# Three chunks in two layers: chunk 0 alone, then chunks 1 and 2 together with seven block products for eight

## The chip, the cores and the metric

The kernel runs on one NeuronCore of one Trainium2 chip. The metric is the device time of one execution in microseconds (us); the time before is the median of three runs. Everything about the insides of an execution comes from one profiled execution of the kernel before.

## What is computed

Block attention with a window and block summaries, followed by two feed-forward layers, all in float32:

```python
x = attention(q, k, v)                    # as (1536 tokens, 512)
g, val = x @ w_gate, x @ w_val            # 512 -> 1536, twice
y = (g * sigmoid(g) * val) @ w_out        # 1536 -> 512
h = y @ w_in                              # 512 -> 2048
out = where(h >= 1, h, where(h <= -1, 0, (h + 1)**2 / 4)) @ w_out2   # 2048 -> 512
```

The attention has batch 2, 8 heads, 768 positions of 64 numbers. The weights arrive as float64 and are decoded on the chip.

## The kernel before

The 1536 tokens are three chunks of 512. A block product takes a 128x128 block of weights (or of the hidden tile) as the stationary operand and 512 columns as the moving one. To keep float32 accuracy each operand is split into a high and a low float32r part, and a block product is three matmuls of 128x512 (high·high, high·low, low·high: `PASSES`, issued by `mm3`, line 888). Per chunk, layer 1 has 12 units f of 128 hidden columns: gate and value products (4 block products each, PSUM tiles `pg`, `pv`), and the output product (`acc_y`, 4 block products). Layer 2 has 16 units: inner (`pi`) and output. That is 816 matmuls of 128x512 per chunk and 2448 in all.

Around the products: two weight units form a pack of 128x1024. A pack is loaded raw (`raw`), decoded on ScalarE and VectorE (`dx`, `dl`, `wb`), written to DRAM in decoded form (`kept_...`), and split into high and low (`wA`, lines 339/343 and 820). Later chunks read the decoded pack back (`wf`) and split it again. Each unit's activation takes ScalarE (tanh or relu, line 925 or 941) and VectorE (lines 931, 936, 955), and its result is split too (`h`). Attention of the later chunks is scattered between the matmuls.

No order is written by hand. A planner (`Plan.emit`) takes jobs with a rank, engine costs, needs and rings of buffers, and issues whichever job can start earliest; the numbers in the table `T` set the ranks, and its `order` says which chunk and layer follow one another: chunk 0 and 1 layer 1, chunk 0 and 1 layer 2, chunk 2 layer 1 and 2. Where the planner expects TensorE to idle in front of a new PSUM bank, `bank` fills in transposes of the identity that nothing reads (line 267), at most ten.

## Time and profile before

| what | value |
|---|---|
| device time, median of 3 runs | 647.35 us (646.94 to 647.78) |
| the profiled execution: device time | 648.05 us |
| the profiled execution: span, first to last instruction | 646.3 us |
| TensorE matmul busy | 634.6 us (98%) |
| VectorE, ScalarE, GpSimd busy | 443.8, 304.4, 46.8 us |
| mean granted TensorE clock | 0.997 |

PE is TensorE's matmuls, DVE is VectorE, ACT ScalarE, POOL GpSimd, SP the engine that issues the DMAs. The profiled execution took 0.70 us more than the median of the runs, and 1.75 us of it lie outside the span.

### The profile page before, as it was taken

How to read it: one execution, taken by the hardware profiler on the slowest of the kernel's cores; microseconds unless marked ns; L12 is line 12 of the kernel's file. 1: busy time of each engine (PE TensorE's matmuls, PEld its weight loads, DVE VectorE, ACT ScalarE, POOL GpSimd, SP SyncE). 2: the span in 40 equal slices, each digit the busy share in tenths (PEclk: the TensorE clock that was granted, in tenths of full speed). 3: DMA queues.
4: the chain of work that ended last, by engine and by line, in shares of the span. 5: the costliest groups of instructions: out<-in, count | busy, mean ns of one | idle time of the engine just before them, and what ended most of it. 6: DMA issues, size and time to landing. Idle time of an engine off the chain costs nothing.

```text
span 646.3 us, 9320 instructions
## 1 busy us (share of the span) xinstructions
PE 634.6 (98%) x3543; PEld 516.0 (80%) x3543; DVE 443.8 (69%) x785; ACT 304.4 (47%) x501; POOL 46.8 (7%) x92
## 2 busy tenths in 40 slices
PE   7999999998999999999999999999999999999997
PEld 6777777776888888888887787778888888888886
DVE  5798978887755568987867667675565555756552
ACT  5696787775422225667644545353322222533332
POOL 7420003222000000000000100000000000000000
PEclk9999999998999999999999999999999999999999
DMA  9999999269523335699722422221523332323201
GB/s 208 277 331 275 371 368 300 92 213 315 218 98 98 98 124 193 239 241 375 276 98 84 161 66 87 95 82 65 188 74 97 98 97 99 112 84 109 87 1 65
DMA packets 78348, 105.99 MB, mean 164 GB/s; under 512 B 36832, under 2 KB 59360, under 8 KB 78304
## 3 DMA queue, kind: packets, MB, share of 16 engines
q1 hardware_dynamic: 78304, 105.40, 51.7%
q8 instruction: 28, 0.46, 0.3%
q14 instruction: 16, 0.13, 0.1%
HBM read 84.41 MB, written 20.97 MB: 163 GB/s over the span
## 4 chain that ended last, share of the span: by engine, by line
PE 91%; DMA 3%; DVE 2%; SPq 1%; ACT 1%; issue 1%; POOL 0%; DVEq 0%; POOLq 0%; ACTq 0%
PE acc_y L888 36%; PE pi L888 20%; PE pg L888 14%; PE pv L888 14%; PE px L505 2%; PE sc L549 1%; DMA kraw<-in_k_dram 1%; DMA kept_g<-wb 1%; PE pt L605 1%; PE pv L423 1%; DMA vrest<-in_v_dram 1%; SPq L363 1%; DVE wb L797 1%; PE pq L489 0%; PE pk L452 0%
## 5 line engine op out<-in xcount | busy, mean ns | idle before, releaser
L888 PE MATMUL acc_y<-wA,h 128*128 128x512 f32 x576 | 140.5, 393 | 0.0
L888 PE MATMUL pi<-y,wA 128*128 128x512 f32 x576 | 139.3, 391 | 0.0
L888 PEld LDWEIGHTS pi<-y,wA 128*128 128x128 f32 x576 | 107.5, 188 | 22.8 <-issue 0.6
L888 PEld LDWEIGHTS acc_y<-wA,h 128*128 128x128 f32 x576 | 107.0, 188 | 22.5 <-issue 0.5
L888 PE MATMUL pg<-x,wA 128*128 128x512 f32 x432 | 108.7, 398 | 1.9 <-POOL wA L820 1.8
L888 PE MATMUL acc_y<-h,wA 128*128 128x512 f32 x432 | 106.1, 394 | 0.6 <-DVE u L936 0.4
L888 PE MATMUL pv<-x,wA 128*128 128x512 f32 x432 | 106.1, 392 | 0.4 <-DVE x L518 0.4
L888 PEld LDWEIGHTS pg<-x,wA 128*128 128x128 f32 x432 | 81.2, 191 | 20.2 <-POOL wA L820 2.2
L888 PEld LDWEIGHTS acc_y<-h,wA 128*128 128x128 f32 x432 | 80.1, 188 | 18.7 <-DVE u L936 0.9
L888 PEld LDWEIGHTS pv<-x,wA 128*128 128x128 f32 x432 | 80.5, 188 | 17.5 <-DVE x L518 0.8
L820 DVE TENSOR_TENSOR wA<-wf,wA 128x1024 fp32r<-128x1024 f32 x68 | 83.4, 1226 | 6.0 <-ACT wA L339 3.7
L339 ACT ACTIVATE wA<-wf 128x1024 fp32r<-128x1024 f32 x37 | 39.3, 1062 | 88.5 <-PE acc_y L888 57.3
L941 ACT ACTIVATE r<-pi,half_b 128x512 f32<-128x512 f32 x48 | 33.0, 688 | 95.7 <-PE pi L888 95.6
L955 DVE SCALAR_TENSOR_TENSOR r<-pi,r 128x512 f32<-128x512 f32 x48 | 33.0, 687 | 29.1 <-ACT r L947 29.0
L925 ACT ACTIVATE u<-pg 128x512 f32<-128x512 f32 x36 | 21.6, 600 | 62.3 <-PE pg L888 62.2
L931 DVE SCALAR_TENSOR_TENSOR u<-u,pg 128x512 f32<-128x512 f32 x36 | 24.7, 686 | 37.3 <-ACT u L925 37.2
L936 DVE TENSOR_TENSOR u<-u,pv 128x512 f32<-128x512 f32 x36 | 24.7, 687 | 33.9 <-PE pv L888 33.7
L797 DVE SCALAR_TENSOR_TENSOR wb<-dx,dl 128x1024 int32<-128x1024 int32 x34 | 41.3, 1221 | 6.6 <-ACT dl L339 2.1
L343 DVE CAST wA<-wf 128x1024 fp32r<-128x1024 f32 x31 | 22.0, 710 | 33.8 <-PE pi L888 27.6
L786 ACT ACTIVATE dx<-raw 128x1024 f32<-128x1024 f32 x34 | 38.6, 1140 | 5.2 <-DVE wb L797 3.2
L341 POOL TENSOR_SCALAR kwin<-kT 128x96 f32<-128x96 f32 (+2 forms) x40 | 17.0, 442 | 315.1 <-PE sc L549 257.4
L820 DVE TENSOR_TENSOR wA<-wb,wA 128x1024 fp32r<-128x1024 f32 x30 | 36.6, 1221 | 0.5
(92 smaller groups left out, 567.1 us busy)
## 6 DMA issues: line engine op xcount, KB each, us to landing
raw<-in_moe_w_out_dram SPq DMA_DIRECT2D x14, 1024.0 KB, 8.7
wf<-kept_g SPq DMA_DIRECT2D x24, 512.0 KB, 3.3
raw<-in_moe_w_in_dram SPq DMA_DIRECT2D x16, 512.0 KB, 6.7
wf<-kept_i SPq DMA_DIRECT2D x16, 512.0 KB, 3.3
wf<-kept_z SPq DMA_DIRECT2D x16, 512.0 KB, 3.2
raw<-in_moe_w_gate_dram SPq DMA_DIRECT2D x12, 512.0 KB, 7.4
raw<-in_moe_w_val_dram SPq DMA_DIRECT2D x12, 512.0 KB, 8.9
kept_g<-wb SPq DMA_DIRECT2D x12, 512.0 KB, 8.6
```

The costliest lines, as they stand in the source:

```text
L339: nc.scalar.activation(out, in_, AF.Copy, scale=scale)
L341: nc.gpsimd.tensor_scalar(out, in_, scale, 1.0, op0=ALU.mult, op1=ALU.mult)
L343: nc.vector.tensor_copy(out, in_)
L786: nc.scalar.activation(x, raws[k][:, :, :, 1].bitcast(F32), AF.Prelu, scale=2.0 ** -112, alpha=2.0 ** 32)
L797: nc.vector.scalar_tensor_tensor(b, x, 3, words.pop((k, "low")), op0=ALU.logical_shift_left, op1=ALU.bitwise_or)
L820: e.tensor_tensor(out, a, b, op=ALU.subtract)
L888: nc.tensor.matmul(dst, lhs(a), rhs(b), start=first and i == 0, stop=last and i == 2)
L925: nc.scalar.activation(u, banks_of[n], AF.Tanh, scale=0.5)
L931: nc.vector.scalar_tensor_tensor(u, u, 1.0, banks_of[n], op0=ALU.add, op1=ALU.mult)
L936: nc.vector.tensor_tensor(u, u, banks_of[n], op=ALU.mult)
L941: nc.scalar.activation(r, banks_of[n], AF.Relu, bias=half_b, scale=0.5)
L955: nc.vector.scalar_tensor_tensor(r, banks_of[n], 1.0, r, op0=ALU.max, op1=ALU.min)
```

## The change

Chunk 0 goes through both layers as before, in the planner's `units`. Meanwhile the attention of chunks 1 and 2 leaves its results as plain float32 tiles (`flat`). Then chunks 1 and 2 go through both layers together. In gate, value and inner a 2x2 arrangement is formed: two 256-row halves of the contraction, two units f, two chunks. Its eight block products become seven, in Winograd's form of Strassen's scheme (`FORMS`): four combinations of weights (`add_group`, tile `sj`) and four of activations (`add_term`, tile `tj`) are formed by VectorE or GpSimd, both get split (`wjo`, `wjs`, `xj`), and seven products per quad (`form`, tiles `qg`, `qv`, `qi`; six matmuls each) are accumulated in PSUM banks. A running sum in one bank is copied out three times on the way (`fork`), each time before the next product is added to it, and three of the copies get another bank added (`join`). The output products keep eight of eight (`row_jobs`); they read their packs again per chunk (tile `dd`).

Matmuls of 128x512: `pg`, `pv` and `pi` had 432, 432 and 576. Now chunk 0 keeps 144, 144 and 192, and the joint part has 12 gate and value quads and 8 inner quads of 42 matmuls.

To make room, twenty-two 128x512 slots (`s0` to `s21`) replace several pools, `dx` and `dl` share one ring `dd`, PSUM is four banks `b0` to `b3` and four accumulators, and the attention's tiles share memory (`big0`, `big1`) with the split activations of the joint part, which can therefore be written only when all attention is done.

```diff
- 'order': ((0, 1), (1, 1), (0, 2), (1, 2), (2, 1), (2, 2)),
...
+ 'order': ((0, 1), (0, 2)),
...
+    FORMS = {
+        1: ("o", 1, 0), 2: ("o", 2, 1), 3: ("s", 3, 2), 4: ("o", 0, 6),
+        5: ("s", 0, 3), 6: ("s", 1, 4), 7: ("s", 2, 5),
+    }
...
+    SUMS = {0: (0, 1, ALU.add), 2: (2, 0, ALU.subtract), 1: (4, 2, ALU.subtract), 3: (3, 5, ALU.subtract)}
...
+        for s, (x, y, _) in SUMS.items():
+            needs = [("ja", *n)] + [("js", *n, z - 4) for z in (x, y) if z >= 4]
+            job(("js", *n, s), {"DVE+": 0.7, "POOL": 1.32}, t + T["js"][st - 1],
+                lambda e, *_, s=s: add_group(st, i, s, e), needs, (("raw",),) if s == 0 else (),
+                follows=[("js", *n, 0)] if s == 2 else [])
...
+    TERMS = {
+        3: ((C2, 0), (C1, 0)), 5: ((C2, 1), (C2, 0)), 4: ((C2, 1), 3), 6: ((C1, 1), 4),
+    }
...
+    def add_term(st, k, b, engine, ring):
+        x, y = (
+            parts_of[st, k, z] if isinstance(z, int) else flat[st, z[0], k + HALF * z[1]]
+            for z in TERMS[b])
+        t = parts_of[st, k, b] = slot(ring, "tj")
+        (nc.gpsimd if engine == "POOL" else nc.vector).tensor_tensor(t, x, y, op=ALU.subtract)
...
+    def term_hi(st, k, b, engine):
+        if (st, k) not in xts:
+            xts[st, k] = big.tile([P, 7, 2, CH], F32R, tag=f"big{k}", name=f"xj{k}")
+        copy(engine, xts[st, k][:, b, 0], operand(st, k, b))
...
+    def term_lo(st, k, b, engine):
+        t = xts[st, k]
+        subtract(engine, t[:, b, 1], operand(st, k, b), t[:, b, 0].bitcast(F32))
...
+        for b in range(7):
+            c, z = ((C1, 0), (C1, 1), (C2, 1))[b] if b < 3 else (None, None)
+            source = ("f", st, c, k + HALF * z) if b < 3 else ("t", st, k, b)
+            job(("th", st, k, b), {"ACT": 0.64, "DVE+": 0.43}, t + T["th"] + b / 3,
+                lambda e, b=b: term_hi(st, k, b, e), [source, *before])
+            job(("tl", st, k, b), {"DVE+": 0.7, "POOL": 1.32}, t + T["tl"] + b / 3,
+                lambda e, b=b: term_lo(st, k, b, e), [("th", st, k, b)], (),
+                [(source, 0)])
+
+    def form(q, p, first, last, ring=None):
+        st, i, e = q
+        what, x, y = FORMS[p]
+        if ring:
+            quads[q, "acd"[{1: 0, 2: 2, 5: 1}[p]]] = bank(ring, "q" + "gvi"[e if st == 1 else 2])
+        dst = quads[q, {2: "d", 5: "c", 3: "c"}.get(p, "a")]
+        w = split[what, st, i, e]
+        for k in range(HALF):
+            t = xts[st, k]
+            mm3(dst, lambda a: w[:, a, x, k * P:(k + 1) * P], lambda b: t[:, y, b],
+                first and k == 0, last and k == HALF - 1, skip_group_check=not first)
+
+    def fork(q, what, engine, ring):
+        t = quads[q, what] = slot(ring, "q" + what)
+        copy(engine, t, quads[q, "a"])
+
+    def join(q, what, src):
+        nc.vector.tensor_tensor(quads[q, what], quads[q, what], quads[q, src], op=ALU.add)
+
+    def quad_jobs(q, t, slots):
+        st, i, e = q
+        order = dict(zip((1, 2, 6, 5, 7, 4, 3), T["qp"]))
+        waits = {6: [("qf", *q, "s1")], 7: [("qf", *q, "u2")], 4: [("qf", *q, "u3")],
+                 3: [("qj", *q, "u3")]}
+        for p, dt in order.items():
+            what, _, y = FORMS[p]
+            needs = [("gl", what, *q)] + [("tl", st, k, y) for k in range(HALF)] + waits.get(p, [])
+            if p == 1 and q in follow:
+                needs.append(("qp", *follow[q], 1))
+            last = {"o": 4, "s": 3}[what] == p
+            gives = [(("gh", what, *q), 0)]
+            job(("qp", *q, p), {"PE": 6 * MM}, t + dt,
+                lambda eng, *ring, p=p: form(q, p, p in (1, 2, 5), True, *ring),
+                needs, (QB,) if p in (1, 2, 5) else (), gives)
+        for p, what in ((1, "s1"), (6, "u2"), (7, "u3")):
+            job(("qf", *q, what), {"ACT": 0.61, "DVE": 0.7}, t + order[p] + T["qf"],
+                lambda eng, ring, what=what: fork(q, what, eng, ring), [("qp", *q, p)], (slots,))
+        for what, src, p, gives in (
+                ("s1", "d", 2, [(("qp", *q, 2), 0)]), ("u3", "c", 5, []),
+                ("u2", "c", 3, [(("qp", *q, 5), 0)])):
+            job(("qj", *q, what), {"DVE": 0.7}, t + order[p] + T["qj"],
+                lambda eng, what=what, src=src: join(q, what, src),
+                [("qp", *q, p), ("qf", *q, what)], (), gives)
...
+        for c, df, made, key, held in (
+                (C1, 1, ("qj", *q, "s1"), "s1", (("qf", *q, "s1"), 0)),
+                (C2, 0, ("qj", *q, "u3"), "u3", (("qf", *q, "u3"), 0)),
+                (C1, 0, ("qp", *q, 4), "a", (("qp", *q, 1), 0)),
+                (C2, 1, ("qj", *q, "u2"), "u2", (("qf", *q, "u2"), 0))):
+            act_jobs(kind, (c, st, f + df), lambda key=key: quads[q, key], t, made, held, slots,
+                     "DVE" if key == "a" else "DVE+")
...
+    def row_jobs(c, st, f, t):
+        kind, n = "oz"[st - 1], f - f % PACK
+        key = (kind, n, c)
+        if f == n:
+            r = t + T["rw"]
+            job(("f32", key), {"DMA": (0.35, 0.7 * PACK)}, r, lambda *_: read_rows(key),
+                [("keep", kind, n)], (("wf",),), follows=prior("f32", key) or [("bits", len(packs) - 1)])
+            split_jobs(key, r + T["rs"], ("f32", key), "dd")
+        split_hidden((c, st, f), t + T["rh"])
+        parts = [(m,) for m in range(KK)] if f == LAST[st] else [(0, 1), (2, 3)]
+        for i, ms in enumerate(parts):
+            name = ("row", c, st, f, i)
+            gives = []
+            if i == len(parts) - 1:
+                gives = [(("hh", c, st, f), 0)] + ([(("hi", key), 0)] if f > n else [])
+            job(name, {"PE": 3 * MM * len(ms)}, t + i * 2.6 / len(parts),
+                lambda e, *rings, ms=ms: row_use(key, c, st, f, ms, rings),
```

The order of the rows on the engines is the planner's, and so it can't be read off the diff. Three places follow.

TensorE in layer 1 before, in chunk 2: one unit f, with four block products of gate (`pg`), four of value (`pv`) and four of output (`acc_y`), each over the four blocks `x` of the contraction; x3 is the three passes.

```order
L888 MATMUL pg<-x_3491,wA 128x512 x3
L888 MATMUL pg<-x_3763,wA 128x512 x3
L888 MATMUL pg<-x_3978,wA 128x512 x3
L888 MATMUL pg<-x_4206,wA 128x512 x3
L888 MATMUL pv<-x_3491,wA 128x512 x3
L888 MATMUL pv<-x_3763,wA 128x512 x3
L888 MATMUL pv<-x_3978,wA 128x512 x3
L888 MATMUL pv<-x_4206,wA 128x512 x3
L888 MATMUL acc_y_4490<-h,wA 128x512 x3
L888 MATMUL acc_y_4491<-h,wA 128x512 x3
L888 MATMUL acc_y_4503<-h,wA 128x512 x3
L888 MATMUL acc_y_4504<-h,wA 128x512 x3
```

The changed kernel at the corresponding place, where the third of six groups of the joint layer 1 passes into the fourth. A product of a quad is two rows (two blocks `xj`); these are product 7 of the third group's value quad, product 1 of the fourth group's gate quad, products 4 and 3 of the value quad, half an output unit of chunk 1 (`acc_y`), and product 6 of the gate quad.

```order
L933 MATMUL qv<-xj_3011,wjs 128x512 x3
L933 MATMUL qv<-xj_3036,wjs 128x512 x3
L933 MATMUL qg<-xj_3011,wjo 128x512 x3
L933 MATMUL qg<-xj_3036,wjo 128x512 x3
L933 MATMUL qv<-xj_3011,wjo 128x512 x3
L933 MATMUL qv<-xj_3036,wjo 128x512 x3
L933 MATMUL qv<-xj_3011,wjs 128x512 x3
L933 MATMUL qv<-xj_3036,wjs 128x512 x3
L933 MATMUL acc_y_3440<-h,dd 128x512 x3
L933 MATMUL acc_y_3441<-h,dd 128x512 x3
L933 MATMUL qg<-xj_3011,wjs 128x512 x3
L933 MATMUL qg<-xj_3036,wjs 128x512 x3
```

A unit's eight block products before stood in one row of twelve matmuls each, with nothing to wait for between them. Now products 7 and 4 of the value quad go into one running sum that is copied out between them, with one other product in between; products 1 and 6 of the gate quad likewise, with three others.

TensorE where layer 1 ends and layer 2 begins. Before, in chunk 2: the last output products and the first inner ones.

```order
L888 MATMUL acc_y_4490<-h,wA 128x512 x3
L888 MATMUL acc_y_4491<-h,wA 128x512 x3
L888 MATMUL acc_y_4503<-h,wA 128x512 x3
L888 MATMUL acc_y_4504<-h,wA 128x512 x3
L888 MATMUL pi<-y_5006,wA 128x512 x3
L888 MATMUL pi<-y_5013,wA 128x512 x3
L888 MATMUL pi<-y_5019,wA 128x512 x3
```

Now: the last output product of chunk 2, products 1 and 2 of the first two inner quads, seven filler transposes, and the first half of product 5.

```order
L933 MATMUL acc_y_4248<-h,dd 128x512 x3
L933 MATMUL qi<-xj_4227,wjo 128x512 x3
L933 MATMUL qi<-xj_4257,wjo 128x512 x3
L933 MATMUL qi<-xj_4227,wjo 128x512 x3
L933 MATMUL qi<-xj_4257,wjo 128x512 x3
L933 MATMUL qi<-xj_4227,wjo 128x512 x3
L933 MATMUL qi<-xj_4257,wjo 128x512 x3
L933 MATMUL qi<-xj_4227,wjo 128x512 x3
L933 MATMUL qi<-xj_4257,wjo 128x512 x3
L289 MATMUL qi<-ident 128x128 x7
L933 MATMUL qi<-xj_4227,wjs 128x512 x3
```

Layer 2 began with the four blocks `y` in turn; now the first four products need chunk 1 alone, and fillers stand ahead of the first product that needs chunk 2.

VectorE in layer 1 before, in chunk 2, two units f: gate activation, value activation, the split of the hidden tile, the split of weights.

```order
L931 SCALAR_TENSOR_TENSOR u<-u,pg 128x512
L936 TENSOR_TENSOR u<-u,pv 128x512
L343 CAST h<-u 128x512
L820 TENSOR_TENSOR h<-u,h 128x512
L820 TENSOR_TENSOR wA<-wf,wA 128x1024
L931 SCALAR_TENSOR_TENSOR u<-u,pg 128x512
L936 TENSOR_TENSOR u<-u,pv 128x512
L343 CAST h<-u 128x512
L820 TENSOR_TENSOR h<-u,h 128x512
L343 CAST wA<-wf 128x1024
L820 TENSOR_TENSOR wA<-wf,wA 128x1024 x2
```

Now, twelve of the 25 rows that one group of the joint layer 1 has: joins (L1251), a sum of weights (L1142), activations (L976), and the splits of the output pack (`dd`), of plain blocks (`wjo`) and of sums (`wjs`).

```order
L1251 TENSOR_TENSOR qs_3613<-qs_3613,qg 128x512
L1142 TENSOR_TENSOR sj<-wj,sj 128x2x256
L976 SCALAR_TENSOR_TENSOR u<-u,qs_3613 128x512
L1251 TENSOR_TENSOR qu_3694<-qu_3694,qg 128x512
L976 SCALAR_TENSOR_TENSOR u<-u,qu_3694 128x512
L388 CAST dd<-wf 128x1024
L875 TENSOR_TENSOR dd<-wf,dd 128x1024
L875 TENSOR_TENSOR wjo<-wj,wjo 128x768
L1251 TENSOR_TENSOR qu_3652<-qu_3652,qg 128x512
L875 TENSOR_TENSOR wjs<-sj,wjs 128x1024
L1251 TENSOR_TENSOR qs_3713<-qs_3713,qv 128x512
L976 SCALAR_TENSOR_TENSOR u<-u,qg 128x512
```

The activations stand between joins and wait for them, and the weights' splits stand between both. The other 13 rows of the group are two joins, one activation of gate, four of value, one more sum of weights, one cast and two splits of weights, and two splits of the hidden tile.

## Rows read from the trace of the kernel before

**Rows 1.** The page: span, busy time by engine, granted clock by slice, DMA queue.

```profile
span 646.3 us, 9320 instructions
...
PE 634.6 (98%) x3543; PEld 516.0 (80%) x3543; DVE 443.8 (69%) x785; ACT 304.4 (47%) x501; POOL 46.8 (7%) x92
...
PEclk9999999998999999999999999999999999999999
...
q1 hardware_dynamic: 78304, 105.40, 51.7%
```

**Rows 2.** Windows: length; busy of PE, PEld, DVE, ACT, POOL; clock; DMA share; GB/s.

```profile
0.00:60.00 60.00, 54.20 (x546) 44.25 (x547) 45.34 (x130) 41.73 (x61) 23.27 (x63) 1.00 1.06 273
60.00:144.00 84.00, 83.48 (x546) 65.27 (x547) 70.91 (x150) 63.43 (x124) 14.90 (x17) 1.00 0.80 270
...
250.00:330.00 80.00, 80.00 (x357) 66.25 (x356) 65.61 (x82) 53.58 (x64) 0.00 (x0) 1.00 0.82 261
...
450.00:640.00 190.00, 190.00 (x839) 157.35 (x839) 111.23 (x150) 54.12 (x73) 0.00 (x0) 1.00 0.27 89
640.00:646.30 6.30, 2.66 (x12) 1.88 (x10) 0.00 (x0) 2.39 (x4) 0.00 (x0) 1.00 0.45 166
```

**Rows 3.** Timeline of the steady second layer: start, length, engine, line, operation.

```profile
571.78 2.88 PE L888 MATMUL pi<-y,wA 128*128 128x512 f32 x12
...
574.50 2.88 PE L888 MATMUL acc_y<-wA,h 128*128 128x512 f32 x12
574.70 0.69 ACT L941 ACTIVATE r<-pi,half_b 128x512 f32<-128x512 f32 x1 [1.66 <-PE pi L888]
```

**Rows 4.** Groups by shape: busy us, mean ns | idle time before.

```profile
L820 DVE TENSOR_TENSOR wA<-wf,wA 128x1024 fp32r<-128x1024 f32 x68 | 83.4, 1226 | 6.0 <-ACT wA L339 3.7
...
L339 ACT ACTIVATE wA<-wf 128x1024 fp32r<-128x1024 f32 x37 | 39.3, 1062 | 88.5 <-PE acc_y L888 57.3 <-PE pv L888 27.5 <-DMA wf<-kept_g 3.7
...
L820 DVE TENSOR_TENSOR h<-r,h 128x512 fp32r<-128x512 f32 x47 | 32.6, 693 | 1.7
...
L936 DVE TENSOR_TENSOR u<-u,pv 128x512 f32<-128x512 f32 x36 | 24.7, 687 | 33.9 <-PE pv L888 33.7
...
L343 DVE CAST wA<-wf 128x1024 fp32r<-128x1024 f32 x31 | 22.0, 710 | 33.8 <-PE pi L888 27.6 <-PE acc_y L888 5.2 <-DMA wf<-kept_g 1.0
...
L343 DVE CAST h<-u 128x512 fp32r<-128x512 f32 x33 | 14.8, 450 | 1.1
...
L339 ACT ACTIVATE x<-px 128x512 fp32r<-128x512 f32 x12 | 7.2, 598 | 9.7 <-PE px L505 9.7
...
L820 POOL TENSOR_TENSOR h<-u,h 128x512 fp32r<-128x512 f32 x2 | 2.6, 1290 | 9.6 <-DVE h L343 9.2 <-ACT h L339 0.4
```

**Rows 5.** Timeline around the one long wait in mid-kernel.

```profile
148.94 0.73 PE L888 MATMUL pg<-x,wA 128*128 128x512 f32 x2
149.03 2.37 POOL L820 TENSOR_TENSOR wA<-wb,wA 128x1024 fp32r<-128x1024 f32 x1 [5.64 <-ACT wA L339]
...
150.58 1.11 DVE L343 CAST h<-u 128x512 fp32r<-128x512 f32 x1
...
151.46 4.15 PE L888 MATMUL pg<-x,wA 128*128 128x512 f32 x10 [1.78 <-POOL wA L820]
```

**Rows 6.** Windows, columns as in group 2: a wait in the head, the one in mid-kernel.

```profile
14.00:16.00 2.00, 0.88 (x8) 0.68 (x7) 1.52 (x9) 1.34 (x2) 1.81 (x4) 1.00 0.94 162
150.00:151.00 1.00, 0.00 (x0) 0.00 (x0) 0.96 (x2) 1.00 (x7) 1.00 (x1) 1.00 0.94 284
153.00:154.00 1.00, 1.00 (x3) 0.76 (x3) 0.93 (x4) 0.45 (x1) 0.00 (x0) 0.50 1.03 422
```

**Rows 7.** Timeline of TensorE in the head: filler transposes, then a wait.

```profile
11.52 1.53 PE L267 MATMUL sc<-ident 128*128 128x128 f32 x12
...
15.32 0.88 PE L452 MATMUL pk<-ident,kord 128*128 128x128 f32 x6 [1.12 <-ACT kord L339]
```

**Rows 8.** DMA issues: the reads of the decoded gate weights.

```profile
wf<-kept_g SPq DMA_DIRECT2D x24, 512.0 KB, 3.3
```

More of the change, by code (lines that the diff above doesn't have):

```diff
@@ L478, in tile_block_attention_ffn @@
     xt = {}
-    smx = [const.tile([P, WPS, KN + 1], F32, name=f"sm{i}") for i in range(plan.rings["sm"])]
+    JOINT = (1, 2)
     for t in smx:
@@ L840, in prior @@
             return []
-        return [before if isinstance(k, tuple) and k[0] in ("bits", "f32") else (what, before)]
+        return [before if isinstance(k, tuple) and k[0] in ("bits", "f32", "gh", "hh") else (what, before)]
     def load_us(k):
@@ L884, in tile_block_attention_ffn, with mm3 @@
     yt, banks_of, accs, us, hs = {}, {}, {}, {}, {}
-    def mm3(dst, lhs, rhs, first, last):
+    def mm3(dst, lhs, rhs, first, last, **more):
         for i, (a, b) in enumerate(PASSES):
             nc.tensor.matmul(
-                dst, lhs(a), rhs(b), start=first and i == 0, stop=last and i == 2
+                dst, lhs(a), rhs(b), start=first and i == 0, stop=last and i == 2, **more
             )
@@ new lines, in tile_block_attention_ffn, with group_units, read_group @@
+    prior_group = []
+    plain, sums, split, xts, quads, parts_of = {}, {}, {}, {}, {}, {}
+    GROUPS = {1: F1 // 2, 2: F2 // 4}
+    def group_units(st, i, e):
+        return ("gv"[e], 2 * i) if st == 1 else ("i", 4 * i + 2 * e)
+    def read_group(st, i):
+        t = plain[st, i] = wp.tile(
+            [P, 2, 4, 256], F32, tag="raw", name="wj", bufs=plan.rings["raw"])
+        for j in range(2):
+            if st == 1:
+                nc.sync.dma_start(
+                    out=t[:, :, 2 * j:2 * j + 2].rearrange("p e b x -> p e (b x)"),
+                    in_=kept["g", 2 * i + j])
+            else:
+                nc.sync.dma_start(
+                    out=t[:, j].rearrange("p (u b) x -> p u (b x)", u=2),
+                    in_=kept["i", 4 * i + 2 * j])
@@ new lines, in tile_block_attention_ffn, with add_group @@
+    SUMS = {0: (0, 1, ALU.add), 2: (2, 0, ALU.subtract), 1: (4, 2, ALU.subtract), 3: (3, 5, ALU.subtract)}
+    def add_group(st, i, s, engine):
+        w = plain[st, i]
+        if s == 0:
+            sums[st, i] = wp.tile(
+                [P, 2, 4, 256], F32, tag="raw", name="sj", bufs=plan.rings["raw"])
+        both = [w[:, :, x] if x < 4 else sums[st, i][:, :, x - 4] for x in SUMS[s][:2]]
+        (nc.gpsimd if engine == "POOL" else nc.vector).tensor_tensor(
+            sums[st, i][:, :, s], *both, op=SUMS[s][2])
@@ new lines, in group_source, with group_hi, group_lo @@
+    def group_source(what, st, i, e):
+        return plain[st, i][:, e, 1:4] if what == "o" else sums[st, i][:, e]
+    def group_hi(what, st, i, e, engine):
+        n = 3 if what == "o" else 4
+        t = split[what, st, i, e] = wp.tile(
+            [P, 2, n, 256], F32R, tag="wA", name="wj" + what, bufs=plan.rings["wA"])
+        copy(engine, t[:, 0], group_source(what, st, i, e))
+    def group_lo(what, st, i, e, engine):
+        t = split[what, st, i, e]
+        subtract(engine, t[:, 1], group_source(what, st, i, e), t[:, 0].bitcast(F32))
@@ L1085, in tile_block_attention_ffn @@
         use_jobs(n, when(n))
+    QB = BANKS
+    prior_row = []
+    attention = [("av", c, p) for c in JOINT for p in range(NPAIR)]
+    order = [(st, i, e) for st in (1, 2) for i in range(GROUPS[st]) for e in range(2)]
+    follow = dict(zip(order[1:], order))
+    for st in (1, 2):
+        t0, step, half = T["j"][st - 1], T["g"][st - 1], T["q"][st - 1]
+        for kt in range(HALF):
+            before = attention if st == 1 else [
+                ("qp", *q, p) for q in order[-GROUPS[2] * 2 - 2:-GROUPS[2] * 2] for p in FORMS]
+            term_jobs(st, kt, T["x"][kt] if st == 1 else t0 + T["x2"] + kt, before, JS)
+        for i in range(GROUPS[st]):
+            group_jobs(st, i, t0 + step * i + T["jw"][st - 1])
+            for e in range(2):
+                quad_jobs((st, i, e), t0 + step * i + half * e, JS)
+        n = (F1, F2)[st - 1]
+        each = 2 * step / (2 if st == 1 else 4)
+        for f in range(n):
+            row_jobs(C1, st, f, t0 + each * (f // 2 + 1) + T["jr"][st - 1] + UNIT * (f % 2))
+        t0 += each * n / 2 + T["jr"][st - 1] + T["r2"][st - 1]
+        for f in range(n):
+            row_jobs(C2, st, f, t0 + UNIT * f)
     with tc.manual_schedule():
```

471 lines of the change are left out of this document (284 added, 187 removed).

## The prediction

> **What bounds the kernel now.** The page comes first [rows 1]: TensorE's matmuls are busy 634.6 of 646.3 us at almost full granted clock, VectorE 69%, ScalarE 47%, the DMA engines about half. A share is a mean, so the windows come next [rows 2]. TensorE is idle for 5.8 us in the first 60 us and for 0.5 us in the next 84; from 250 to 330 and from 450 to 640 us it never idles. VectorE is at 84% from 60 to 144 us, where weights are decoded and attention runs, and at 59% from 450 to 640. So TensorE is the bound, stage by stage, and time is won by giving it less to do and lost by letting it wait.
>
> The timeline gives the price of its work [rows 3]: twelve matmuls of 128x512 run from 571.78 to 574.50 us, when the next twelve start, 0.2267 us each. (The means in a group of matmuls are latencies and overlap; they don't add up.) The 2448 take 555.0 us of the 634.6; the rest is attention, fillers and one slow stretch.
>
> That stretch is the one long wait after the head [rows 5, 6]. TensorE stood still for 1.78 us behind a weight split on GpSimd, and then ran ten matmuls in 4.15 us where 2.27 are due: the granted clock, 1.00 until then, was 0.50 at 153 us, 1.2 instead of 2.4 GHz. The wait cost 1.78 and the clock behind it another 1.9, 3.7 together. A wait of 1.12 us in the head left the clock at 1.00 [rows 6, 7].
>
> **The change, part by part.** *Removed.* Gate, value and inner of chunks 1 and 2 had 288, 288 and 384 matmuls; twenty quads of 42 are 840, so 120 fall away: 120 x 0.2267 = 27.2 us [rows 3]. They stood on the bound, and nothing hides behind them. Everything else of TensorE stays: 816 matmuls of chunk 0, 672 of the joint output products, attention.
>
> *Fillers.* The order has 75 filler transposes, 47 before. Twelve took 1.53 us [rows 7], so 28 more are 3.6 us. Fifteen of them stand in the head, seven where layer 2 begins. They mark where the order expects TensorE to wait in any case.
>
> *Added for VectorE and GpSimd.* 60 joins (0.687, as a gate product read from PSUM), 40 half-pack sums and 16 activation terms (0.693, as the hidden split), 12 splits more; the weight splits fall from 102 packs to 62 packs, 20 wide tiles and 20 of three quarters, 97 in all [rows 4]: 41.2 + 27.7 + 11.1 + 8.3 - 6.1 = 82 us more. *For ScalarE*: 60 copies from PSUM at 0.598 and 28 more copies and casts, about 53 us. None of it is TensorE's, so it is free as long as TensorE doesn't wait. In the steady part of the joint layer 1 a group of two quads and two output units is 108 matmuls, 24.5 us. VectorE's 25 rows in it: 18 of 0.69, three wide ones of 1.226, two of three quarters (between 0.693 and 1.226; I take 0.95), two casts of 0.71 and about 0.57, together 19.3 us, 79% against 59% before. From 60 to 144 us VectorE ran at 84% with TensorE waiting 0.5 us. So VectorE's volume doesn't pace this stage.
>
> *Copies inside a running sum.* This wait is new: the copy must be done before the next product may add to the bank. There are 60, three per quad. Bounds from rows: a result can be read 0.20 us after its last matmul has made room [rows 3], the copy takes 0.60 [rows 4], and TensorE restarts 0.06 after what it waited for (GpSimd's split ended at 151.40, the matmul began at 151.46 [rows 5]): 0.86 us in all. In the order, 43 of the 60 have at least two products or output halves between, 2.72 us, and can't wait long. Seventeen have one, 1.36 us: half a microsecond to spare, unless ScalarE has just begun a weight cast of 1.06 [rows 4]; then the wait is up to 0.56. From 0 to 17 x 0.56 = 9.5 us; ScalarE is busy some 40% of layer 1 and 75% of layer 2 of the joint part, a cast is one row in four, so I take 2.5.
>
> *The start of the joint part.* Its split activations need all of attention, because they share memory with it. From the last product of chunk 0 to the first product of the second group TensorE has 17.0 us of work; VectorE has 17.1 by its rows, GpSimd 6.3. From 0, if the two engines run side by side, to 5.5, if each GpSimd row holds VectorE up. A row shows the second: a VectorE cast of the hidden tile took 1.11 us at 150.58 while GpSimd split a pack, 0.450 on average [rows 4, 5]. VectorE's rows on PSUM can't be held up in that way, and the wait comes in pieces; I take 1.5.
>
> The Trainium skill (SBUF — State Buffer, "Who interferes with whom") says that VectorE and GpSimd share one port pair as an exclusive lock, which two-input VectorE instructions in SBUF and its two-port casts need as well; the cast at 150.58 agrees. By that rule GpSimd's 32 rows in the joint part, some 45 us, would be added to VectorE's 275, 320 of the 343 us that TensorE has there: no new bound over the whole, but 5.5 us at the start instead of 1.5, and the sum 4 us higher.
>
> *The start of layer 2.* The first four products (5.4 us) need chunk 1 only. Meanwhile four results are copied out, combined, cast and split; for the first product on chunk 2 about seven VectorE rows of 0.69 stand in the queue behind 0.8 us of copying, 5.6 us, against 5.4 + 1.4 of work and 0.9 of fillers. From 0 to 3; I take 1.
>
> *Chunk 0's stage.* All decoding and all attention now fall before the joint part. Transfers: 51.7% of the span is 334 us of DMA time [rows 1]. From 450 to 640 us there are only reads of decoded packs and stores: 17 MB in 51 us [rows 2], 3.0 us per MB. The 68 half-megabyte reads of such packs (24 of gate [rows 8], 44 others) and 3 MB of output thus take 117; the other 217 us must now fit into some 270 us of TensorE's work (185 for chunk 0, the 79.6 besides the matmuls, 5.8 idle in the head), a share of 0.80, as from 60 to 144 and 250 to 330 us, where TensorE ran through [rows 2]. From 0 to 8 (217 us bunched as in the head, at a share of 1.06); I take 1.
>
> **The sum**, against the profiled execution's 648.05: - 27.2 + 3.6 + 2.5 + 1.5 + 1 + 1 = 630.45; the median of the runs stood 0.70 below, so 629.8, rounded to 629.5.
>
> **The rivals.** *Nothing is lost* beside the work, and the wait at 150 us goes too, since chunk 0's order is another: 648.05 - 27.2 - 3.7 + 3.6 - 0.7 = 620. For it speaks that the order before left one stall in 580 us; against it, seventeen new narrow places.
>
> *The copies pace the joint part.* Every second of the 60 waits 0.56, and the start costs 5.5: 17 + 5.5 in place of 4, some 648; half as bad, 639. For it: layer 2 has ScalarE at 75% and four narrow copies in a row right at its start. Against it: 43 of the 60 have two products between.
>
> *Chunk 0's stage is stretched* by transfers or by VectorE, by up to 8 us: 637.
>
> *Slower, through the clock.* If waits in the joint part reach the 1.78 us of the row at 150 us, each costs 3.7 instead of its own length. The gain left after fillers is 23.6; it decides from seven such places on. One in each of layer 2's eight quads, and at both starts, would be 37 us: 660. For it: the clock fell in the only such case that the trace has. Against it: a narrow copy makes 0.56, and 1.12 in the head did no harm.
>
> **How the numbers follow.** The forecast, 624 to 637: 0.60. Nothing lost, 616 to 624: 0.12. Copies pace it, 637 to 648: 0.14. Chunk 0's stage stretched, 634 to 640: 0.05. Slower, through the clock, 648 to 670: 0.09. The range of 8 in 10 is 619 to 643: it leaves out the slow case, a third of the lower one and the upper third of the copies. A change of 0.2% (1.3 us) is about what a measurement of this kernel can tell from none. Faster by more: 0.89; the same: 0.03; slower: 0.08.
>
> **What would show it.** Right: 2328 matmuls of 128x512, still 2.72 us per twelve; TensorE busy some 610 us; waits of products on copies (`qs`, `qu`) of tenths of a microsecond; VectorE near 80% in the joint part and never the last to end for long. Wrong: a granted clock below 1.0 in the joint part, waits of over a microsecond there, a window before 270 us in which DMA is at 1.0 and TensorE idles, or a span of chunk 0's stage beyond 275 us.

## The result, and the profile after

The changed kernel takes 632.65 us (632.12 to 633.20, four runs) against 647.57 (646.94 to 650.41); the ratio is 0.9761, 95% interval 0.9731 to 0.9792. It is 2.4% faster. The forecast was 629.5 in a range of 619 to 643: the sign and the size hold, and some 3 us of the expected 18 did not come. The profiled execution takes 632.74 us, 1.74 of them outside its span.

The page of the changed kernel, the lines that answer to [rows 1]:

```profile
span 631.0 us, 9313 instructions
...
PE 611.4 (97%) x3451; PEld 496.4 (79%) x3451; DVE 491.3 (78%) x842; ACT 372.9 (59%) x624; POOL 116.0 (18%) x128
...
PEclk9998999999999999999899999999999999999999
```

TensorE has 92 instructions fewer than in [rows 1], which is 120 matmuls less and 28 fillers more, and is busy 23.2 us less. But it idles 19.6 us (631.0 - 611.4) against 11.7 before. So the question is where 8 us of new idle time stand. The windows answer to [rows 2], with the same columns:

```profile
0.00:60.00 60.00, 51.77 (x555) 42.58 (x556) 43.77 (x145) 39.36 (x72) 31.71 (x63) 0.97 0.99 256
60.00:144.00 84.00, 82.75 (x459) 65.43 (x458) 71.29 (x114) 64.17 (x100) 17.49 (x18) 1.00 0.99 325
144.00:275.00 131.00, 129.82 (x921) 103.11 (x920) 109.18 (x229) 104.24 (x207) 16.64 (x18) 1.00 0.66 213
275.00:320.00 45.00, 41.60 (x174) 33.14 (x173) 40.02 (x47) 22.32 (x37) 18.07 (x11) 0.96 0.26 94
320.00:460.00 140.00, 140.00 (x619) 115.63 (x618) 109.96 (x147) 52.74 (x78) 18.41 (x11) 1.00 0.23 78
460.00:480.00 20.00, 18.18 (x84) 14.89 (x83) 17.68 (x27) 14.83 (x26) 1.73 (x1) 1.00 0.09 35
480.00:624.00 144.00, 144.00 (x637) 119.21 (x636) 99.38 (x139) 72.90 (x107) 11.98 (x7) 1.00 0.16 55
...
309.00:310.00 1.00, 0.46 (x1) 0.42 (x2) 1.00 (x2) 1.00 (x2) 0.00 (x0) 0.83 0.00 0
310.00:313.00 3.00, 3.00 (x8) 2.30 (x7) 2.03 (x4) 0.64 (x2) 0.00 (x0) 0.50 0.00 0
```

From 320 to 460 us and from 480 to 624 us TensorE never idles, and 619 matmuls in 140 us are what 0.2267 each allows (617.6). The new idle time stands in three places: the first 60 us (8.2, against 5.8 before), 275 to 320 us (3.4), where the joint part starts, and 460 to 480 us (1.8), where its layer 2 starts. Between 60 and 275 us it is 2.4, against 2.3 before. The list of TensorE's waits (us in total, times, longest) names what it waited for:

```profile
PE qg L933 <- DVE qu L1251: 2.9, 2, 2.1
PE pg L933 <- DVE xl L565: 2.8, 1, 2.8
...
PE qi L289 <- DVE qs L1251: 1.8, 1, 1.8
```

The first and third are joins of half results (`qu`, `qs`) on VectorE, the second is the split of an attention output in the head. No wait on a copy (`qu` or `qs` by ScalarE) is in the list at all. The timeline shows the three places, and one more near 94 us; the columns are those of [rows 3]:

```profile
45.07 2.52 POOL L875 TENSOR_TENSOR wA<-wb,wA 128x1024 fp32r<-128x1024 f32 x1 [1.04 <-ACT wA L384]
45.28 3.38 DVE L852 SCALAR_TENSOR_TENSOR wb<-dd 128x1024 int32<-128x1024 int32 x1
49.32 0.50 PE L933 MATMUL pg<-xl,wA 128*128 128x512 f32 x1 [2.76 <-DVE xl L565]
...
93.35 2.39 POOL L875 TENSOR_TENSOR wA<-wb,wA 128x1024 fp32r<-128x1024 f32 x1 [6.48 <-ACT wA L384]
93.58 3.25 DVE L852 SCALAR_TENSOR_TENSOR wb<-dd 128x1024 int32<-128x1024 int32 x1 [0.20 <-DVE dd L390]
97.48 0.50 PE L933 MATMUL pg<-x,wA 128*128 128x512 f32 x1 [1.25 <-DVE u L976]
...
282.83 1.67 PE L933 MATMUL qg<-xj,wjs 128*128 128x512 f32 x6 [0.46 <-DVE qs L1251]
294.88 1.66 PE L933 MATMUL qg<-xj,wjo 128*128 128x512 f32 x6 [0.81 <-DVE qu L1251]
297.77 3.27 POOL L875 TENSOR_TENSOR h<-u,h 128x512 fp32r<-128x512 f32 x2 [4.36 <-ACT h L384]
299.68 0.69 DVE L1251 TENSOR_TENSOR qs<-qs,qg 128x512 f32<-128x512 f32 x1 [0.46 <-ACT qs L384]
300.29 1.83 DVE L875 TENSOR_TENSOR wjs<-sj,wjs 128x1024 fp32r<-128x1024 f32 x1
301.00 3.98 POOL L1142 TENSOR_TENSOR sj<-wj 128x512 f32<-128x512 f32 x2
302.04 3.48 DVE L976 SCALAR_TENSOR_TENSOR u<-u,qu 128x512 f32<-128x512 f32 x2
304.94 1.73 POOL L1142 TENSOR_TENSOR sj<-sj,wj 128x512 f32<-128x512 f32 x1
305.45 3.44 DVE L979 TENSOR_TENSOR u<-u,qu 128x512 f32<-128x512 f32 x2
306.75 1.59 POOL L1142 TENSOR_TENSOR sj<-wj,sj 128x512 f32<-128x512 f32 x1
308.82 0.67 DVE L1251 TENSOR_TENSOR qu<-qu,qg 128x512 f32<-128x512 f32 x1
309.55 2.84 PE L933 MATMUL qg<-xj,wjs 128*128 128x512 f32 x6 [2.13 <-DVE qu L1251]
...
467.80 1.27 DVE L1251 TENSOR_TENSOR qs<-qs,qi 128x512 f32<-128x512 f32 x2
468.52 0.98 PE L289 MATMUL qi<-ident 128*128 128x128 f32 x7 [1.81 <-DVE qs L1251]
```

In the head, VectorE's joining of a pack's bits (`wb`) takes 3.38 us at 45.28 and 3.25 at 93.58, each beside a weight split on GpSimd; at 77.41, without one, it takes 1.23. TensorE waits 2.76 and 1.25 us behind them. From 301.00 to 308.34 us GpSimd adds half packs, and two VectorE rows that take 0.69 each alone take 1.7 each. The join at 308.82 stands behind four such rows in VectorE's queue, and TensorE behind the join. After it six matmuls take 2.84 us instead of 1.52. The last two windows show why: the granted clock, 1.00 until then, is 0.50 from 310 to 313 us, 1.2 instead of 2.4 GHz.

### The profile page after: what moved, and what is told of

Read it like the earlier page. It is cut to its first block, busy times and chain, and to the rows that moved or that the text cites. A ratio compares the mean times of both kernels' runs of the same rounds, so it can differ in the third digit from the quotient of the medians.

```text
span 631.0 us, 9313 instructions
## 1 busy us (share of the span) xinstructions
PE 611.4 (97%) x3451; PEld 496.4 (79%) x3451; DVE 491.3 (78%) x842; ACT 372.9 (59%) x624; POOL 116.0 (18%) x128
## 4 chain that ended last, share of the span: by engine, by line
PE 84%; DVE 6%; DMA 3%; ACT 2%; SPq 2%; issue 2%; DVEq 0%; ACTq 0%
PE acc_y L933 35%; PE qi L933 12%; PE qv L933 8%; PE qg L933 8%; PE pi L933 7%; PE pg L933 4%; PE pv L933 4%; PE px L552 2%; DMA raw<-in_moe_w_val_dram 2%; PE sc L602 1%; DVE wb L852 1%; PE pt L658 1%; PE pv L470 1%; SPq L432 1%; DMA vrest<-in_v_dram 1%
## 5 line engine op out<-in xcount | busy, mean ns | idle before, releaser
L933 PE MATMUL acc_y<-dd,h 128*128 128x512 f32 x384 | 89.3, 389 | 0.0
L933 PEld LDWEIGHTS acc_y<-dd,h 128*128 128x128 f32 x384 | 72.1, 188 | 15.0
L933 PE MATMUL acc_y<-h,dd 128*128 128x512 f32 x288 | 68.2, 389 | 0.0
L933 PEld LDWEIGHTS acc_y<-h,dd 128*128 128x128 f32 x288 | 54.1, 188 | 11.3
L933 PE MATMUL acc_y<-wA,h 128*128 128x512 f32 x192 | 47.4, 395 | 0.0
L933 PE MATMUL pi<-y,wA 128*128 128x512 f32 x128 | 44.8, 402 | 0.0
L933 PEld LDWEIGHTS acc_y<-wA,h 128*128 128x128 f32 x192 | 35.4, 188 | 7.8 <-issue 0.6
L933 PE MATMUL acc_y<-h,wA 128*128 128x512 f32 x144 | 35.6, 395 | 0.0
L933 PE MATMUL pg<-x,wA 128*128 128x512 f32 x96 | 34.3, 406 | 1.2 <-DVE u L976 1.2
L933 PEld LDWEIGHTS qg<-xj,wjs 128*128 128x128 f32 x144 | 27.4, 193 | 9.6 <-DVE qu L1251 2.5
L933 PE MATMUL pv<-x,wA 128*128 128x512 f32 x96 | 33.6, 401 | 0.0
```

The source lines that it names most:

```text
L933: nc.tensor.matmul(dst, lhs(a), rhs(b), start=first and i == 0, stop=last and i == 2, **more)
```

## The experiments

**Theory:** the saving of 27.2 us is real, the copies inside the running sums cost nothing, and the shortfall is a matter of VectorE's queue at the two starts of the joint part, where GpSimd's rows hold VectorE's rows up; the clock adds to it. **Rivals:** the copies (or ScalarE) pace the joint part; VectorE's plain volume does, GpSimd being harmless; the fillers cost what the prediction gave them; the head is set by transfers and decoding.

Experiments that move or reassign single steps keep the planner's order and change only what is named, by this hook:

```diff
+    def run(self, name, engine, fn, chosen):
+        if name in self.LATER:
+            return self.PARKED.setdefault(self.LATER[name], []).append((name, engine, fn, chosen))
+        self.pad = self.PADS.get(name, self.pad)
+        fn(self.FORCE.get(name, engine), *chosen)
+        for x in self.PARKED.pop(name, ()):
+            x[2](self.FORCE.get(x[0], x[1]), *x[3])
...
-            fn(engine, *chosen)
+            self.run(name, engine, fn, chosen)
```

All results together. The last three columns are read from TensorE's timeline of each profiled run: the start of the first joint product (`qg`), from there to the first product of layer 2 (`qi`), and from there to the end of the span. They tell the stages apart where the ratio can't.

| kernel | median us | ratio to before, 95% interval | first joint product | joint layer 1 | layer 2 to end |
|---|---|---|---|---|---|
| changed kernel | 632.65 | 0.9761 (0.9731 to 0.9792) | 272.7 | 188.45 | 169.9 |
| the same once more | 631.33 | 0.9737 (0.9709 to 0.9765) | 272.8 | 186.9 | 169.9 |
| one product of each quad twice | 652.80 | 1.0058 (1.0045 to 1.0072) | 273.0 | 199.6 | 178.8 |
| VectorE's order at the start | 630.48 | 0.9711 (0.9693 to 0.9728) | 273.75 | 185.1 | 170.0 |
| nine GpSimd rows on VectorE | 627.55 | 0.9670 (0.9657 to 0.9684) | 273.0 | 182.6 | 169.9 |
| VectorE's order in the head | 631.60 | 0.9733 (0.9719 to 0.9746) | 273.6 | 186.9 | 169.9 |
| copies twice | 635.04 | 0.9787 (0.9770 to 0.9804) | 272.6 | 188.6 | 171.5 |
| copies three times | 649.20 | 1.0015 (1.0004 to 1.0025) | 273.6 | 193.7 | 180.7 |
| no fillers | 631.47 | 0.9730 (0.9712 to 0.9748) | 272.0 | 186.9 | 169.2 |
| both starts | 627.03 | 0.9665 (0.9647 to 0.9684) | 273.8 | 182.6 | 168.4 |
| both starts and the head | 626.54 | 0.9661 (0.9635 to 0.9687) | 275.2 | 182.6 | 168.4 |
| these, no GpSimd in the joint part | 625.38 | 0.9644 (0.9618 to 0.9670) | 271.7 | 182.3 | 168.5 |
| both starts and the head, no fillers | 624.91 | 0.9635 (0.9609 to 0.9661) | 273.0 | 182.6 | 168.5 |

**One product of each quad twice.**

```diff
-        for k in range(HALF):
+        for k in (*range(HALF), *range(HALF if p == 1 else 0)):
```

> Each of the twenty quads makes its first product twice (the second pass starts the bank afresh, so the values stay), and with that has as many matmuls as before the change: 120 more, in the changed order of work. Theory: TensorE is the bound all through the joint part, so these cost their own time, 120 x 0.2267 = 27.2 us: 632.65 + 27.2 = 659.9, if no wait is covered by them; at most some 4 us less if the longer quads swallow the waits at the two starts. Rival, copies and VectorE pace the joint part: the added matmuls fill waits that are there anyway, and the time comes to 645 to 652.

Measured: 652.80 us, by the ratios 19 to 21 us above the changed kernel's two measurements: short of the theory's number, and at the upper edge of the rival's. The stages tell which is right. The rival's steady waits are nowhere: 620 matmuls stand between 320 and 460 us, as before. The joint part is 378.4 us long (199.6 + 178.8). Against the changed kernel (358.3) that is 20.0, because the waits of 2.13 and 1.81 us and the half clock are gone: TensorE, with one product more in each quad, no longer overtakes VectorE at the two starts. Against 351.0 in the kernel further down in which both starts are mended it is 27.4, close to the 27.2 of 120 matmuls (the kernel with the product twice still has a wait of 0.67 and 0.7 of fillers there). So the work saved is worth its time, and taking it away is what opened the waits.

**VectorE's order at the start.** `u2` and `u3` are the activation rows that hold the queue in the timeline above, `qj` the join.

```diff
+    LATER = {('u2', 2, 1, 1): ('qj', 1, 1, 0, 'u3'), ('u3', 2, 1, 0): ('qj', 1, 1, 0, 'u3'),
+             ('u3', 2, 1, 1): ('qj', 1, 1, 0, 'u3')}
```

> On VectorE, three activation rows of the first quads (2 of the third group of four rows at 302 to 308.8 us among them) go behind the join of the third quad's half result on which TensorE waited 2.13 us at 309.55. Theory: that wait is one of order on VectorE, and the granted clock of 0.50 behind it goes with it: the wait of 2.13 and 1.8 us of slow matmuls disappear, 632.65 - 3.9 = 628.8; up to 1 us may come back as a wait on the rows that were put back. Rival, VectorE is short at this place by its whole volume: the wait only moves to the next joins, and the time stays at 632 to 633.5.

Measured: 0.9711, some 3 us less than the first measurement of the changed kernel, and the joint layer 1 is 3.4 us shorter. The wait of 2.13 and the half clock are gone, and one of 0.27 came at 312.90; waits of 0.47 and 0.83 at 284 and 296 us stay, as no row there was moved. Against the second measurement, in whose profile the clock stayed at 1.00 behind the same wait, the gain is 1.7 us by the ratio, with overlapping intervals, and 1.8 in the joint layer 1.

**Nine GpSimd rows on VectorE.** `js` adds half packs, `lo` splits a pack, `hl` a hidden tile.

```diff
+    FORCE = {('js', 1, 1, 2): 'DVE', ('js', 1, 1, 3): 'DVE', ('lo', ('o', 2, 1)): 'DVE',
+             ('hl', 1, 1, 0): 'DVE', ('hl', 1, 1, 1): 'DVE', ('js', 1, 2, 0): 'DVE',
+             ('js', 1, 2, 2): 'DVE', ('js', 1, 2, 1): 'DVE', ('js', 1, 2, 3): 'DVE'}
```

> Nine of GpSimd's rows between 289 and 309 us (six sums of half packs, a weight split, two splits of the hidden tile) are made by VectorE in the same place of its queue; nothing else changes. Theory, GpSimd's rows hold VectorE's up: VectorE gets 6.6 us of rows (8 x 0.68 + 1.22), 3.5 of them ahead of the join at 309, but loses the stretch of its own rows (3.03 for 0.95, 3.48 and 3.44 for 1.3 each, 1.83 for 1.21, 1.13 for 0.55: 7.4 us), so the join comes earlier, the wait of 2.13 shrinks below 1 and the clock stays at 1.00: 629 to 631.5. Rival, VectorE's volume: the rows were long for another reason, the join comes 3.5 us later, the wait grows to about 5.6 us and the time to some 636.

Measured: 627.55, ratio 0.9670, below even the theory's range, and clear of both intervals of the changed kernel. The joint layer 1 is 5.85 us shorter than in its first profile and 4.3 shorter than in the second, where the clock stayed at 1.00. (One of the nine rows stands ahead of the 289 us that the expectation names, at 279.28.) VectorE has nine rows more to do and is done earlier. Its timeline at the same place:

```profile
300.72 1.29 DVE L976 SCALAR_TENSOR_TENSOR u<-u,qu 128x512 f32<-128x512 f32 x2
301.93 1.28 DVE L979 TENSOR_TENSOR u<-u,qu 128x512 f32<-128x512 f32 x2
303.81 0.69 DVE L1251 TENSOR_TENSOR qu<-qu,qg 128x512 f32<-128x512 f32 x1 [0.59 <-ACT qu L384]
...
305.70 1.52 PE L933 MATMUL qg<-xj,wjs 128*128 128x512 f32 x6
```

The two pairs of activation rows take 1.29 and 1.28 us, not 3.48 and 3.44; the join comes 5 us earlier, and TensorE does not wait for it, nor anywhere between 275 and 320 us. This decides between the theory and VectorE's volume.

**VectorE's order in the head.** `bits` is the row of 3.38 us at 45.28, `xl` the split that TensorE waited for.

```diff
+    LATER = {('bits', 2): ('xl', 0, 2)}
```

> In the head, VectorE's joining of a pack's bits at 45.28 us (3.38 us long beside a GpSimd weight split of 2.52) goes behind the split of the third attention output, on which TensorE waited 2.76 us at 49.32. Theory: wait and slow clock behind it (matmuls at 0.50 to 0.67 until 54 us, 1.7 us) go: 632.65 - 4.4 = 628.2, less what the later bits cost (up to 1): 628.2 to 629.3. Rival, the head is set by the transfers and the decoding of the first packs: the wait moves to the next pack and the time stays at 632 to 633.

Measured: 0.9733, which is 1.8 us below the changed kernel's first measurement and level with its second. The wait of 2.76 us went, one of 1.54 came at 50.18 and one of 1.81 at 79.98, with the clock at 0.50 behind it; the first joint product comes no earlier (273.6). The rival holds for the head as a whole.

**Copies twice, three times.** Nothing but the copies of running sums is repeated.

```diff
         copy(engine, t, quads[q, "a"])
+        copy(engine, t, quads[q, "a"])
```

> Each of the 60 copies of a running sum from PSUM is made twice over, in the same place (60 ScalarE rows of 0.60 us more, nothing else). Theory, the copies cost nothing as they are: two copies in a row take 1.07 us, so with 0.26 around them 1.33 of the 1.36 us that the seventeen narrow places have; the time rises by 0 to 2 us over the changed kernel (632.65 there). Rival, the copies already pace the joint part or its layer 2, where ScalarE is busiest: each second copy adds to the wait, 10 us and more.

> The same with three copies for one. Theory: 0.26 + 1.6 = 1.86 us against 1.36 in the seventeen narrow places, 0.5 each, 8.5 us together over the changed kernel (5 to 13 with the rows that queue behind the copies on ScalarE); the 43 wide places (2.72 us) still hide them. Here the granted clock may fall behind the waits, each is short. If the time still does not rise, the cover is wider than worked out from the order; if it rises by 25 or more, ScalarE as a whole paces.

Measured: 635.04 and 649.20, by the ratios 2 to 3 and 16 to 18 us above the changed kernel's two measurements. Two copies cost the most that the theory allowed or a little more; three cost more than it said. The waits of TensorE in the kernel with three copies:

```profile
PE qi L933 <- ACT qu L384: 6.4, 10, 1.4
PE qv L933 <- ACT qu L384: 3.5, 6, 0.6
```

In layer 1 they recur with each group at 0.59 us, close to the 0.5 worked out. In layer 2, where copies also queue behind other ScalarE work, they reach 1.4, and that stage grows by 10.8 us, layer 1 by 5 to 7. One copy fits into 1.36 us, the second reaches its edge, the third does not fit: so the copies as they are cost nothing, with about half a microsecond to spare.

**No fillers.** In the hook, in place of the line with `PADS`:

```diff
+        self.pad = 0
```

> All 75 filler transposes are left out. They stand for 75 x 0.128 = 9.6 us of TensorE work. Theory: most stand where TensorE would wait anyway, in the head behind transfers; only the seven at layer 2's start (0.98 us behind a wait of 1.81 that they cannot begin before, since they write the bank that the wait frees) and a few of the head's lie on the path: the time falls by 1 to 3 us below the changed kernel. Rival, as the prediction put it, all 28 added ones are on the path: 3.6 us and more. Other rival: without them the head's granted clock falls, and the time rises by 2 or more.

Measured: 0.9730, by the ratios 2.0 us less than the first measurement of the changed kernel, 0.5 less than the second; its interval overlaps both. The first joint product comes 0.7 us earlier, and layer 2 is 0.7 shorter (the seven fillers begin only behind the wait that they were to fill, at 468.52). By these medians seventy-five fillers cost 0.5 to 2 us, not 9.6. The mean granted clock of the first 60 us is 0.94 here and 0.97 in the first profile with fillers, but that is not the fillers' doing: in both it is 1.00 up to 45 us and falls at the wait of 2.76 near 49, and the second profile of the changed kernel, with its fillers, has 0.94 as well.

**Both starts.** The nine rows as above, and at layer 2's start (`hi` casts a pack, `qf` copies, `t`, `th` and `tl` make a term, cast and split it):

```diff
+    FORCE = {..., ('t', 2, 1, 4): 'DVE'}
+    LATER = {('hi', ('z', 2, 1)): ('qf', 2, 0, 1, 's1'), ('tl', 2, 0, 5): ('qj', 2, 0, 1, 's1'),
+             ('t', 2, 0, 6): ('qj', 2, 0, 1, 's1'), ('t', 2, 1, 4): ('qj', 2, 0, 1, 's1'),
+             ('th', 2, 0, 6): ('qj', 2, 0, 1, 's1')}
+    PADS = {('qp', 2, 0, 0, 5): 0}
```

> The nine GpSimd rows of the joint part's start are made by VectorE, as in the run before that was 5.9 us below the changed kernel by its ratio; besides, at the start of layer 2 a weight cast on ScalarE goes behind two copies, four rows of VectorE and ScalarE (a term and what splits it) go behind the two joins on which TensorE waited 1.81 us, one GpSimd term is made by VectorE, and the seven fillers behind the wait are left out. Theory: the wait of 1.81 is one of order and shrinks to 0.7 or less, the fillers' 0.98 go, some 2 us below the run before, ratio 0.963 to 0.965. Rival, VectorE is short there by its volume: the wait comes back at the products on the rows that were put off (products six and seven), and only the fillers' 0.98 is gained, 0.9655.

Measured: 0.9665, level with 0.9670, yet layer 2 to the end is 1.5 us shorter (168.4 instead of 169.9). Its timeline shows the wait of 1.81 replaced by two small ones, on the put-off terms:

```profile
465.80 0.50 PE L933 MATMUL qi<-xj,wjs 128*128 128x512 f32 x1 [0.44 <-ACT xj L384]
466.60 4.88 PE L933 MATMUL qi<-xj,wjs 128*128 128x512 f32 x20 [0.30 <-DVE xj L875]
```

Most of the wait was order. Of the 1.5 us, 0.7 are the fillers, as the run without fillers shows, and 0.8 the order. The theory's ratio of 0.963 to 0.965 was not reached. In the two profiles the first joint product came 0.8 us later here, which takes half of the gain back; the ratios do not resolve the rest.

**The head, GpSimd left out, fillers left out.** Four kernels on one chip, the changed one among them. To the edit above come, in turn (the list of the 32 steps is written short):

```diff
+    FORCE = {..., ('lo', 1): 'DVE'}
...
+    FORCE = {all 32 GpSimd steps of the joint part: 'DVE', ('lo', 1): 'DVE'}
...
+        self.pad = 0
```

> The changed kernel once more, unchanged, for the comparison with the three that follow on the same chip: a ratio of 0.976 within its interval of 0.973 to 0.979. In the profile the wait of about 2.1 us near 309 us is due again in every account; if the granted clock behind it stays at 1.00 this time, as in two other runs, the part from the first joint product to layer 2 is 186.9 us long, if it falls 188.4.

> The kernel with both starts reordered (ratio 0.9665 before), and in the head the GpSimd weight split at 45 us, beside which VectorE's joining of bits took 3.38 us instead of 1.2, is made by VectorE in its place in the queue. Theory, GpSimd holds VectorE up there too: the bits take 1.2 to 1.5, the split on which TensorE waited 2.76 us comes at 47.2, the wait shrinks to 0.7 and the clock behind it stays up: 2 to 3.8 us less, ratio 0.961 to 0.963. Rival, the head is set by transfers and decoding: the wait goes elsewhere in the head and the first joint product still starts at 273 to 274 us, ratio 0.966.

> The same, and all 32 GpSimd rows of the joint part (some 45 us by their durations) are made by VectorE, in their places: some 24 us of rows more for VectorE in 343 us, 80% to 85% busy there. Theory, VectorE's volume does not pace the joint part, order and GpSimd's hold-up at its start do: no new wait above 0.5 us, the same time as the kernel before it in this list within 1 us. Rival, VectorE needs GpSimd's help: waits on joins in the middle of layer 1 and in layer 2, 3 us and more slower.

> The kernel with both starts and the head changed, without any filler transposes. Theory: in the head they cost about 1 us more than the waits that they fill, so 0.5 to 1.5 us less than with them, and the granted clock of the head does not change. Rival: without them TensorE's clock falls in the head's waits and the time rises by 1 to 3 us.

Measured: 0.9737, 0.9661, 0.9644 and 0.9635. In the head the theory holds for the place and fails for the time. The timeline of the second of the four:

```profile
45.27 1.22 DVE L852 SCALAR_TENSOR_TENSOR wb<-dd 128x1024 int32<-128x1024 int32 x1
...
47.14 0.50 PE L933 MATMUL pg<-xl,wA 128*128 128x512 f32 x1 [0.60 <-DVE xl L565]
...
74.19 1.12 ACT L843 ACTIVATE dd<-raw 128x1024 f32<-128x1024 f32 x1 [5.49 <-DMA raw<-in_moe_w_out_dram]
77.53 1.23 DVE L852 SCALAR_TENSOR_TENSOR wb<-dd 128x1024 int32<-128x1024 int32 x1 [5.23 <-ACT dd L384]
79.40 0.50 PE L933 MATMUL pg<-x,wA 128*128 128x512 f32 x1 [1.93 <-DVE u L976]
...
94.40 2.39 POOL L875 TENSOR_TENSOR wA<-wb,wA 128x1024 fp32r<-128x1024 f32 x1 [7.31 <-ACT wA L384]
94.50 3.38 DVE L852 SCALAR_TENSOR_TENSOR wb<-dd 128x1024 int32<-128x1024 int32 x1 [0.20 <-ACT wA L384]
...
97.80 0.68 DVE L976 SCALAR_TENSOR_TENSOR u<-u,pg 128x512 f32<-128x512 f32 x1
98.53 0.67 PE L933 MATMUL pg<-x,wA 128*128 128x512 f32 x1 [2.15 <-DVE u L976]
```

The bits take 1.22 us with GpSimd away, and the wait at 47 is 0.60. But at 79 TensorE waits for an activation row that stands in VectorE's queue behind a decoding row, this one behind ScalarE, and ScalarE for 5.49 us behind a load of weights. So 1.93 us of what is won at 49 goes to a load. The wait of 2.15 at 98 has another cause: the activation row that TensorE waits for stands behind a joining of bits that takes 3.38 us beside GpSimd's next weight split, the same hold-up as at 45. The changed kernel has it too (3.25 us at 93.58, a wait of 1.25). No run moved that split or changed a load, so it stays open how much of the head is set by its loads. The two kernels with this head and the fillers reach the first joint product at 275.2 and 271.7 us, eight runs with the changed kernel's head at 272.6 to 273.8.

Without any GpSimd row in the joint part nothing is lost: layer 1 takes 182.3, layer 2 168.5, and TensorE's only waits there are two, of 0.4 and 0.3 us. VectorE's volume does not pace the joint part even when it does everything. From the first joint product on it is busy 268.2 us for 388 rows, against 269.4 for 359 in the changed kernel: its rows are no longer stretched, so GpSimd's help had saved it next to nothing. The last kernel, without fillers, is the fastest of the four by its median, 624.91 against 631.33 for the changed one (the ranges, 624.52 to 626.22 and 629.98 to 634.32, don't touch); the intervals of the three mended kernels overlap, and which of them is best is not settled. In the profile of the last one the granted clock was 0.50 from 22 to 27 us, behind a wait of 1.67 at 20.00, as the rival had it; in the other kernel without fillers it stayed at 1.00 behind a wait of 1.66 at the same place.

## Why the prediction was right, and where its terms were off

*The removed matmuls, 27.2.* Right: 27.4 between two kernels whose joint parts wait for 0.7 us each, the longer one with 0.7 of fillers besides. Twelve matmuls still take 2.72 us.

*The copies inside running sums, 2.5.* Too high: 0. The margin of 0.5 us was worked out rightly (the second copy just uses it up). The fear that a weight cast stands ahead on ScalarE did not come true: ScalarE is busy 38% in the joint layer 1, as forecast, but 51% in layer 2 (72.9 of 144 us), not 75%.

*The start of the joint part, 1.5.* This is the term that was too small, and the step that failed is where its stretch ends. The prediction weighed the queues up to the first product of the second group, the matmul at 294.88 us. Up to there the changed kernel takes 22.2 us from its first joint product, against 20.45 with nine GpSimd rows moved: 1.8 lost, close to 1.5. But for the second group the prediction put the loss at nothing, since VectorE's share of a group is 79%. There six more GpSimd rows (297.77 to 308.34 us) stretch four VectorE rows ahead of one join, and TensorE waits 2.13 us at 309.55. The second group on costs 2.5 in the second profile, and the half clock behind the wait another 1.55 in the first. In all the joint layer 1 is 4.3 us longer than with the nine rows moved, 5.85 with the half clock. (The upper bound does not come out of its own figures: 17.1 + 6.3 - 17.0 is 6.4, not 5.5.)

The reason given for the low value was that VectorE's rows on PSUM can't be held up. That agrees with the trace: the join at 299.68 took 0.69 us beside GpSimd's splits. But in the joint part three of a quad's four results lie in SBUF after their joins, so their activation rows (`u<-u,qu`) read two SBUF tiles, where before they read one in PSUM. And the waits were not only small pieces (0.46 and 0.81). The Trainium skill (SBUF — State Buffer, "Who interferes with whom") says that a VectorE instruction with two inputs in SBUF contends with a GpSimd instruction that reads SBUF, and that one with at most one SBUF input, outside its two-port modes, does not. Both halves agree with these rows (1.7 us for 0.69, and the join's 0.69). The prediction's estimate by that rule, 5.5, was nearer to the whole loss than 1.5.

*The start of layer 2, 1 and 0.9 of fillers.* Near: a wait of 1.81 and 0.7 of fillers, 2.5 in place of 1.9, of which the run with both starts won back 1.5.

*The other fillers, 2.7, and chunk 0's stage, 1.* Together 3.7, and what is left of the span's 15.3 is about 3.5 (27.2 less 15.3 is 11.9, less 5.9, less 2.5). But the shares were wrong: all fillers together cost 0.5 to 2 us by the medians, and the stall of 3.7 us at 150 us, which the sum had left in place, went while other losses came in the head (2.76 us, the clock at 0.50 until 54 us, and 1.25 at 97.48). The prediction had priced chunk 0's stage by its transfers. From 60 to 144 us the DMA engines run at 0.99 and TensorE idles for 1.25 us, so transfers did not stretch it by much. What it did not weigh is GpSimd: its first weight split began at 103.10 us before the change, and now five begin from 32.72 to 93.35, two of them beside VectorE's stretched joining of bits.

*The sum* lay within 3 us in part by luck: 2.5 too much for the copies and a stall that went set off what was missing at the start and in the head. Two of the signs that the prediction named for being wrong did show in the joint part, a granted clock of 0.50 and waits of over a microsecond (2.13 and 1.81).

*VectorE's volume.* Right: 78.5% from 320 to 460 us (109.96 of 140), 79% worked out, with no wait.

*The rivals.* "Nothing is lost" was too hopeful for the kernel as it is. The last kernel of the table, with both starts and the head changed and no fillers, takes 624.9, 5 us above that rival's 620; its joint part waits for 0.7 us, so most of the rest must lie ahead of it. "The copies pace it" fell. Of "chunk 0's stage is stretched" the waits on VectorE in the head are seen, not its 8 us. The slower rival's mechanism was seen, once in the joint part and not seven times.
